# Casting loads for V and K, f32 loads for q, and new instruction lists in a chunk-selecting attention kernel with an ELU layer behind it

## The chip, the core and the metric

The kernel runs on one core of a Trainium2 chip. A core has a matrix engine (TensorE, PE in the profile, with its weight loads as PEld), a vector engine (VectorE, DVE), a scalar engine (ScalarE, ACT), a general engine (GpSimd, POOL) and a queue for transfers (SyncE, SP). Each runs its own list of instructions in order and waits on semaphores for the others. Transfers run on 16 DMA engines. SP and ACT issue plain transfers; GpSimd issues the ones that change the type on the way. The metric is device time in microseconds (us), the median of the runs shown.

## The reference

Four batches, eight heads, 768 positions, head width 64. The keys lie in 24 chunks of 32. For each query an upper bound of its score with every chunk is taken from the chunk's minimum and maximum; of the chunks not later than its own it keeps the six with the largest bound. Softmax attention runs over the kept keys that are not later than the query. The result goes through two dense layers with an ELU between them.

```
k_min, k_max = min and max of k over each chunk
ub  = sum_d max(q_d * k_min_d, q_d * k_max_d)          # chunks later than the query's own: -1e9
sel = the 6 chunks with the largest ub
s   = where(key's chunk in sel and key <= query, q.k / 8, -1e9)
x   = softmax(s) @ v                                   # heads side by side: 3072 x 512
out = elu(x @ w_in) @ w_out                            # w_in 512 x 2048, w_out 2048 x 512
```

All inputs and the output are f32 in memory; the matrix work is done in bf16 apart from transposes and bounds.

## The kernel before

**Units.** A unit is 384 query rows. Units 0 and 1 are the two 192-row halves (called p and s) of the first 384 positions of batches 0 and 1; units 2 and 3 are the second 384 positions of batches 0 and 1; units 4 to 7 are the two halves (h 0 and 1) of batches 2 and 3. Heads go in four pairs r, and pairs in two groups G.

**Per unit.** q and k are transposed so that the head width lies on partitions. For batches 0 and 1 TensorE does it (`prep_pair` L423 and L408, `prep` L564) and DVE takes chunk minima and maxima from the transposed keys (L371). For batches 2 and 3 `keys` (L476) casts each 128-row block of k from its f32 landing buffer into a `kt` tile (`kb`), writes the block's chunk marks beside it (`ky`) and has a transposing DMA put it into the score operand `lhs` (`kd`); the minima and maxima come from a second read of k in chunk form (`kc`, L503 to L523). `select` (L600) makes the bounds (L613), finds the sixth largest (L632) and writes a mask row for each query. Scores (L713, L749, L803), exponentials on ACT (L721, L756, L818, L822), a triangular mask on the diagonal blocks (`tri`, L761 and L835, DVE or POOL: a multiplication with a stored triangle), the product with V (L775, L854), the division (L657, L667), and a turn of the result into the first layer's operand `xt` (L690, from unit 4 on a transposing DMA, L678).

**V.** `load_v` (L465) reads a block of V as f32 by SP into a buffer of class `f`, and `v` (L337 on POOL, L324 on ACT, L326 on DVE) casts it into the product's operand `vext`, which holds a whole batch and has two buffers, so batch 2 takes batch 0's.

**The layers.** `mlp` (L865) does for each unit 16 hidden groups `h` (four matmuls of 384 columns, L872), the exponential `e` on ACT (L879), `m` = exp - 1 on POOL or DVE (L881), `g` on DVE (L885, the bf16 tile `gT`), and for each of three row tiles four output groups `o` (four matmuls of 512 columns, L896). The weights are read and cast to bf16 by POOL's transfers (L295 in three pieces, L301 in four).

**The start.** For the p halves q is read and cast by POOL (`wq`, L388) into the first half of an `f` buffer and transposed as bf16 (L408); k is read as f32 by SP and ACT. 22 `fill` matmuls on zeros (L952) stand among the first instructions of TensorE.

**What sets the order.** Nothing is scheduled at run time. `ORDER` is a written list of (engine, operation), and `PLACES` gives each new buffer its slot in its class, with the number of slots in `BUFS`. The framework adds the waits that follow from reads, writes and the reuse of a slot. So each engine runs its part of the list, and what stands behind a waiting instruction waits too.

Of the kernel before, what the change touches and what calls it, by code (L numbers as in the profile page):

```python
# [9 lines left out]
AOT = mybir.AluOpType  # L10
# [29 lines left out]
G0vS0UD00D01PjXA02D09PjYS0sPjZG0wD06Pj-D0iPj+S0uPk0G0aPk1D0oS0rPk2A0TD0jG0kPk3A0tPk4S0XD03G04Pk5  # L40
Pk6Pk7Pk8D05G0bP1mD0lG0cG0WP1hP1nPk9S2dG0eG0pG0VPkaPkbPkcP0KA0OD0PPkdPkeG0nG0gG0fS2fPkfPkgD0qD0m
P18P0RP0IG0dD0SD0MP0BS0zA0JA1cP0+P1iD0CS0xA0FD19P1oP1jS0ZD10D1aD13S2eD0LS2gA1qA1pA15D11GmCP16P1f
P1sS2MA1lGmBD0ND0DD0GS2PS2tP1xA1gD17G0AG08G0yP1wA1kD12P1rP1yS2ND0QP1tA1AGmDP1VA1vA1zD0-P1BP1CP1W
D1DP24P23D25A1uG0YP27P28D26G07D1EG1eP1PP1GD29P1QP1-D1XA2aG0EP1ZD1+D20P1MP1FP1LG2hD1HP2bG1bG2QD1R
P2zD1IA1YP2mD2AP1JD2nP2HP21S2GD1ND1OA1SP1TA2qD2oS2OA1KD22P2uD1UA2cPmYG0HG2sA2ID2BG0hD2pG2CPn4AmZ
Dm-Dm+Pn0An5PmUGn6An1D2vA2JGmEPmQD2wAmVDbqP3jDn7Gn2Dn3A2DS2RAmRGmWPn8A2rG14D3lA1dPmIG2xAn9D3kD3m
GmFA2yPmMD3nPngGnaDmXAmNGmSDnbAmJPnEA2KGmODmTPnsPnAAnhGmGD3oA2FAnFGmKDniPnkD3pGmHDmPA3qA3sPnoDnj
G3rAntP3FDmLAnpGnGPncA3GGnuDnHPnOAnBGnqDnvAndGnCS2kDnrAnlP3+PnwGneA40DnDS2iP3HDnfP36D38A3IP2VD37
P3ZA3tG2LP4jPnIA3-D2XD2WA2ZS4ZPnPA2EG39GnmA2+G2YP4BA3aDnnPnVA4CD41A4kP4DA4EP31P4hP3ePnJA3fD32D33
A4iAnxGnyD4FPnQD34D3gP3uG3JG35DnzG3cG3bPnWA2SD3wS3dA2-D3vD3yD3xA3iS30PnXPnYD3zD2lS2TG2jD3AA3BPnR  # L50
S4-PnKS4YAnSD3ES4XP3LD3CP4MA3hD4lD3DA4NP42DnZP46S4VP3KP43P4GP48A47P4HG2UP4KA49D4IP3QD4JPnLS4WA4L
# [12 lines left out]
DaWD8lD8EGpEDpFAcWGpQDpRDbmG8nG8qA84A8FDd3ApLDpMDpNPpGPpyApjGpkDplAprP8ID8KD8JScSSaBSaCSpbSaHShF
ApHApzA8HAbnG85GpsG8uD8MDptGpIDpJA81AcYGd0GpADpBPqaAqbPpuPpmApnGpoDppDc+ApvGpwDpxAbpD8LPpSApTDpU
PpWPqeApXGqcD8NA86GpYDpZPq2Pp-Pq6PqiPqjPquPqvD8OScZGc-AbjAaIAq3Ap+Aq7DpVGq0Dq1Dq4Dq5DqdA8PP8TP98
PqkGq8Dq9Ad2AqfGqgDqhSboSaJGaKA8UP99A8GA9aD9bP95A96P8VA8WPqwP8XA8YP91A92P93A94P8ZA8-PqxP8+A90D8R
D8SDaVD8QP9iP9mPakP9wD8vGaXA9jA9xSaDPbxP9uAbyDqyPqlA9vAalD97P9dP9cP9qP9sP9zP9kSfpScRGd5ScTSflSd1
ScUDqmA9nA9tP9AA9BGhID9yD9eD9fA9lA9rP9VA9WPqoD9CPaYP9gD9hP9oA9pP9NPbCA9OP9DPamAanP9PP9-P9EP9+A9Q
P9XPqpP9TGaoAa0A9YDb5GbADbDDb4SblSpaSb6D9FD9GDbFDaZPaeP9JP9RPapP9LA9UA9SDa-D9ZPqqPaaPacPaqDa1A9M  # L70
Pa3A9KPa2Dg0Dd6Db7Db8AafAadAarAabPagPaiAajAahPa8Aa9PdnPbsAbtPbHGasPauPatP9HDa4Da5Pa6PqrGfmAbEAbI
A9IAhGAa+Aa7DbaDb9DavDawAfqAqsDbzDbbDbcDbJPaxDayPd8GbdDd9GdcGdbShBSd4DhCSfnDbwDb0DfoSfrPqEAqFGqG
PqIPbeShvAqJDqKAbfAbuPr8Ar9AbgAbhGraAbGDqHDqLSbrSd7SffSqtDrbDfsGbLPrcArdAbiAhOGreDrfPrkArlPqUAqV
AbvPrgPbMDbNGqWDqXDbOArhAhHProAdaGrmDrnDbPGriDrjGg6DbQPr0PqMPqAGbKArpAbBGrqDrrAr1Gr2AqNGqOAdoAqB
PqQAqRGqSAf+DbRDr3DbSDqPPddAdePrwArxPdiAdjPqYAqZGqCDqDDftDqTGbTGryPr4PrsAbVAr5DbWGq-Dq+DfvPrAPbZ
# [926 lines left out]
```

## Time and profile before

| what | value |
|---|---|
| median of 3 runs | 281.37 us (280.41 to 283.12) |
| the profiled execution | 281.2 us, of which the span is 279.5 us |
| TensorE busy | 267.7 us, 96% of the span |
| VectorE, ScalarE busy | 217.2 us, 217.0 us, 78% each |
| GpSimd busy | 128.1 us, 46% |
| bytes moved | 38.07 MB, mean 136 GB/s |
| granted TensorE clock, mean | 0.98 |

The span is the time between the first and the last instruction of the profiled execution; 1.7 us of that execution lie outside it. A busy share is that of the whole span. A wait is put down to the engine and line that ended it. A DMA share above 1 in a stretch means that the 16 engines' packets overlapped each other there.

### The profile page before, as it was taken

What the parts mean: (1) busy time and instruction counts of PE and PEld (TensorE: products, weight loads), DVE (VectorE), ACT (ScalarE), POOL (GpSimd) and SP (SyncE); (2) the same over time, 40 slices, a digit from 0 to 9 for tenths busy, and PEclk for the clock granted to TensorE, in tenths of its full rate; (3) what the DMA queues carried; (4) which work ended last, traced back from release to release, by engine and by line L of the source; (5) the groups of instructions that cost most, each with busy time, mean ns of one, the idle gap of its engine ahead of it and who ended that gap; (6) DMA issues with size and microseconds to landing.
All of it is one profiled execution on the core that took longest, in us unless ns stands there. A gap on an engine that the chain in (4) does not pass through costs nothing.

```text
span 279.5 us, 6962 instructions
## 1 busy us (share of the span) xinstructions
PE 267.7 (96%) x2458; PEld 165.3 (59%) x2458; DVE 217.2 (78%) x655; ACT 217.0 (78%) x491; POOL 128.1 (46%) x256
## 2 busy tenths in 40 slices
PE   7669999999999999999999999999999999999995
PEld 4457555785466855576655555666655556665553
DVE  4957986889978999789998999579797698424931
ACT  2656987889789998999999859886968579982620
POOL 8883954258522665321585736212541346310410
PEclk9876999999999999999999999999999999999999
DMA  9999999999219899965965589317500210033002
GB/s 147 211 195 210 224 197 185 216 237 248 53 59 220 233 236 196 211 150 111 192 169 114 116 218 224 69 41 135 164 4 1 58 39 4 14 126 90 20 11 101
DMA packets 103747, 38.07 MB, mean 136 GB/s; under 512 B 95136, under 2 KB 99488, under 8 KB 103712
## 3 DMA queue, kind: packets, MB, share of 16 engines
q1 hardware_dynamic: 95696, 32.75, 55.4%
q0 software_dynamic: 6832, 4.59, 10.9%
q10 hardware_dynamic: 1184, 0.30, 0.5%
q8 instruction: 19, 0.31, 0.5%
q14 instruction: 16, 0.13, 0.2%
HBM read 30.41 MB, written 6.29 MB: 131 GB/s over the span
## 4 chain that ended last, share of the span: by engine, by line
PE 75%; DVE 8%; ACT 5%; POOL 2%; issue 2%; DMA 1%; DVEq 0%; ACTq 0%; POOLq 0%
PE bank L896 25%; PE bank L872 24%; PE bank L803 10%; PE bank L854 5%; PE bank L613 3%; PE bank L564 2%; DVE gT L885 2%; ACT pt L818 1%; POOL m L881 1%; PE bank L914 1%; PE bank L690 1%; PE bank L423 1%; ACT e L879 1%; PE bank L775 1%; PE bank L749 1%
## 5 line engine op out<-in xcount | busy, mean ns | idle before, releaser
L872 PE MATMUL bank<-xt,w_in_sb 128*128 128x384 bf16 x512 | 90.2, 328 | 0.3 <-DMA xt<-on 0.2
L896 PE MATMUL bank<-w_out_sb,gT 128*128 128x512 bf16 x368 | 89.3, 379 | 0.0
L881 POOL TENSOR_SCALAR m<-e 128x384 f32<-128x384 f32 x100 | 52.0, 529 | 62.0 <-ACT e L879 51.5
L885 DVE SCALAR_TENSOR_TENSOR gT<-bank,m 128x384 bf16<-128x384 f32 x128 | 65.7, 549 | 9.7 <-POOL m L881 8.4
L879 ACT ACTIVATE e<-bank 128x384 f32<-128x384 f32 x128 | 59.1, 493 | 16.0 <-PE bank L872 13.0
L872 PEld LDWEIGHTS <-w_in_sb 128*128 128x128 bf16 x512 | 49.7, 98 | 35.5 <-issue 4.6
L818 ACT ACTIVATE pt<-bank 128x384 bf16<-128x384 f32 (+1 forms) x144 | 67.1, 547 | 3.6 <-PE bank L803 2.5
L896 PEld LDWEIGHTS <-gT 128*128 128x128 bf16 x368 | 34.6, 97 | 36.1 <-issue 2.2
L803 PE MATMUL bank<-rhs,lhs 96*128 96x384 bf16 (+2 forms) x240 | 42.8, 293 | 1.0 <-DVE on L667 0.5
L835 POOL TENSOR_TENSOR pt<-pt,tri 128x256 bf16<-128x256 bf16 (+1 forms) x18 | 16.4, 916 | 38.5 <-ACT pt L822 23.9
L803 PEld LDWEIGHTS <-lhs 96*128 96x128 bf16 x240 | 21.7, 97 | 13.9 <-issue 0.9
L854 PEld LDWEIGHTS <-pt 128*128 128x128 bf16 x576 | 21.0, 97 | 3.6 <-ACT pt L818 0.2
L854 PE MATMUL bank<-vext,pt 128*128 128x65 bf16 x576 | 22.1, 193 | 0.0
L667 DVE TENSOR_TENSOR on<-bank,rcp 128x384 bf16<-128x384 f32 (+1 forms) x37 | 18.7, 510 | 1.3
L326 POOL CAST rhs<-qt 64x384 bf16<-64x384 f32 x24 | 12.8, 539 | 11.8 <-ACT qt L324 10.8
L324 ACT ACTIVATE o<-bank 128x512 f32<-128x512 f32 (+1 forms) x14 | 8.1, 588 | 13.0 <-PE bank L896 10.1
L657 DVE RECIPROCAL rcp<-bank 128x6 f32<-128x6 f32 (+1 forms) x40 | 7.2, 185 | 13.5 <-PE bank L854 9.0
L371 DVE TENSOR_REDUCE kst<-bank 128x12 f32<-128x384 f32 x32 | 16.5, 548 | 1.3 <-ACT kt L324 0.7
L326 DVE COPY o<-bank 128x512 f32<-128x512 f32 (+1 forms) x11 | 7.2, 665 | 12.2 <-PE bank L896 10.0
L835 DVE TENSOR_TENSOR pt<-pt,tri 128x512 bf16<-128x512 bf16 (+1 forms) x30 | 11.2, 390 | 5.4 <-ACT pt L822 3.6
L324 ACT ACTIVATE rhs<-qt 64x384 bf16<-64x384 f32 x28 | 14.2, 518 | 0.5
L822 ACT ACTIVATE pt<-bank 128x512 bf16<-128x512 f32 x24 | 14.0, 604 | 0.7 <-PE bank L803 0.4
(105 smaller groups left out, 340.1 us busy)
## 6 DMA issues: line engine op xcount, KB each, us to landing
f<-in_v_dram SPq DMA_DIRECT2D x22, 256.0 KB, 4.6
out_dram<-o SPq DMA_DIRECT2D x21, 256.0 KB, 3.4
f<-in_q_dram SPq DMA_DIRECT2D x18, 256.0 KB, 4.7
f<-in_k_dram SPq DMA_DIRECT2D x18, 256.0 KB, 4.6
kc<-in_k_dram SPq DMA_DIRECT2D x8, 384.0 KB, 3.9
w_out_sb<-in_moe_w_out_dram POOLq DMA_DIRECT2D x4, 512.0 KB, 9.0
w_in_sb<-in_moe_w_in_dram POOLq DMA_DIRECT2D x2, 512.0 KB, 8.6
w_in_sb<-in_moe_w_in_dram POOLq DMA_DIRECT2D x1, 1024.0 KB, 13.6
```

The source lines that it names most:

```text
L324: nc.scalar.activation(out=dst, in_=src, func=AF.Copy)
L326: eng[e].tensor_copy(out=dst, in_=src)
L667: nc.vector.tensor_tensor(out=ap(on)[:, 0:nt].rearrange("p q h d -> p h q d"), in0=view()[:, :, :, 0:D], in1=ap(rcp)[:, :, 0:nt].to_broadc ...
L803: nc.tensor.matmul(ap(banks[hd])[:, o + pc:o + pc + wd], lhsT=apl(ls, G)[0:96, pr, hd, P * kb:P * (kb + 1)], rhs=ap(rs)[0:96, hd, c0 - HS ...
L818: lambda e, hd=hd, pt=pt, banks=banks, wtot=wtot: nc.scalar.activation(out=ap(pt)[:, hd, PAD:PAD + wtot], in_=ap(banks[hd])[:, 0:wtot], fu ...
L835: eng[e].tensor_tensor(out=view, in0=view, in1=tri[:, 64:64 + P].rearrange("p (a b w) -> p a b w", a=1, b=1) .to_broadcast([P, 2, len(dg), ...
L854: nc.tensor.matmul(view()[:, hd, qi, :], lhsT=ap(pt)[:, hd, P * qi + off:P * qi + off + P], rhs=ap(vx[b])[:, kb, 2 * r + hd, :], start=(kb ...
L872: nc.tensor.matmul(ap(bank)[:, 0:HS], lhsT=w_in_sb[:, kk, P * fc:P * (fc + 1)], rhs=ap(xT[i, kk]), start=(kk == 0), stop=(kk == NKK - 1))
L879: g.op(f"e{i}.{fc}", (ACT,), lambda e, eb=eb, bank=bank: nc.scalar.activation(out=ap(eb), in_=ap(bank)[:, 0:HS], func=AF.Exp), reads=[(ban ...
L881: g.op(f"m{i}.{fc}", (POOL, DVE), lambda e, eb=eb, mb=mb: eng[e].tensor_scalar(out=ap(mb), in0=ap(eb), scalar1=-1.0, scalar2=1.0, op0=AOT. ...
L885: nc.vector.scalar_tensor_tensor(out=ap(gt), in0=ap(bank)[:, 0:HS], scalar=0.0, in1=ap(mb), op0=AOT.max, op1=AOT.min),
L896: nc.tensor.matmul(ap(bank), lhsT=ap(gts[fc])[:, P * tt:P * (tt + 1)], rhs=w_out_sb[:, fc, :], start=(fc == 0), stop=(fc == NFC - 1))
```

## The change

- **V** of all batches: `load_v` no longer reads f32 by SP and casts. GpSimd issues one casting transfer (`wv`) for each of the 26 blocks, straight into `vext`. The 26 f32 loads and the 26 casts are gone. A transfer into a slot of `vext` has to wait until the slot's former batch has been read for the last time.
- **K** of batches 2 and 3: 12 casting transfers (`wk`) into the `kt` tiles take the place of 12 f32 loads and 12 casts `kb`. `ky` and `kd` stay.
- **q** of the p halves: read as f32 by SP, in place of the four casting transfers `wq`; its transposes run in f32 (the path of L423) in place of bf16. Batch 0's are split in two by heads, like its k.
- **The triangular mask** where GpSimd does it in `attend`: one index select for each diagonal block, with zero written below the diagonal, in place of a multiplication with the stored triangle. DVE's stay.
- **Buffers**: `f` 11 to 9 slots, `gT` 17 to 22.
- **The lists** `ORDER` and `PLACES` are new from the first entry to the last, with other choices of engine: `m` 92 on POOL and 36 on DVE (100 and 28 before), `oh` (the 24 one-hot memsets and one clear) on DVE in place of POOL, `qa` 17 on POOL, 9 on DVE, 30 on ACT (24, 4, 28 before), `on` 39 on DVE and 1 on ACT (37 and 3 before), and others by ones and twos. The number of matmuls of the layers, the scores and the products with V is the same, and 22 fills as before. POOL issues 45 transfers (11 before: `wq` 4, weights 7), SP 32 fewer.

```diff
-BUFS = dict(f=11, ..., gT=17, o=3)
+BUFS = dict(f=9, ..., gT=22, o=3)
...
-                    if (n, u) == ("q", 0):
-                        g.op(f"wq{b}{x}", (POOL,), lambda e, buf=buf, x=x: nc.gpsimd.dma_start(
-                            out=short(buf)[0:T96].rearrange("p (h d) -> p h d", d=D),
-                            in_=q[b, :, T96 * x:T96 * (x + 1)].rearrange("h p d -> p h d")),
-                            writes=[(buf, i) for i in range(NG)], dma=True)
-                        continue
...
-        g.op("qT" + tag, (PE,), tr16 if u == 0 else tr(bq, qf),
-             reads=[(f, G) for f in qf] + [(fixed, "idb" if u == 0 else "idf")], writes=[(bq, 0)])
+        g.op("qT" + tag, (PE,), tr(bq, qf), reads=[(f, G) for f in qf] + [(fixed, "idf")],
+             writes=[(bq, 0)])
...
     def load_v(tag, b, kb, p0, p1):
-        vf = Buf("f")
...
-        dma(lambda: (rows(), v[b, :, P * kb + p0:P * kb + p1].rearrange("h p d -> p h d")),
-            [(vf, 0)], [], f"ldv{tag}")
-        vcast(f"v{tag}", lambda: ap(vx[b])[p0:p1, kb, :, 0:D], rows,
-              [(vf, 0)], [(vx[b], (kb, y, r)) for r in range(NPAIR)
...
+        g.op(f"wv{tag}", (POOL,), lambda e: nc.gpsimd.dma_start(
+            out=ap(vx[b])[p0:p1, kb, :, 0:D], in_=v[b, :, P * kb + p0:P * kb + p1].rearrange("h p d -> p h d")),
+            reads=[(fixed, "vo")],
+            writes=[(vx[b], (kb, y, r)) for r in range(NPAIR)
...
-    def keys(b, h, kf):
+    def keys(b, h):
...
-            g.op(f"kb{tag}{x}", (POOL, DVE, ACT), lambda e, kp=kp, x=x: copy(
-                e, ap(kp)[:, :, 0:D], ap(kf[x]).rearrange("p (h d) -> p h d", h=H)),
-                reads=[(kf[x], 0)], writes=[(kp, 0)])
+            t1 = HS * h + P * x
+            g.op(f"wk{tag}{x}", (POOL,), lambda e, kp=kp, t1=t1: nc.gpsimd.dma_start(
+                out=ap(kp)[:, :, 0:D], in_=k[b, :, t1:t1 + P].rearrange("h p d -> p h d")),
+                writes=[(kp, 0)], dma=True)
...
                 def mask(e, pt=pt, dg=dg):
+                    if e == POOL:
+                        for pc in dg:
+                            part = ap(pt)[:, :, PAD + pc:PAD + pc + P]
+                            nc.gpsimd.affine_select(out=part, in_=part, compare_op=AOT.is_ge, fill=0.0, base=0,
+                                                    pattern=[[0, 2], [1, P]], channel_multiplier=-1)
+                        return
```

More of the change, by code (lines that the diff above doesn't have):

```diff
@@ L332, in halves @@
         return ap(bank)[:, 0:HS].rearrange("p (a s) -> p a s", a=2)
-    def vcast(name, dst, src, reads, writes):
-        def emit(e):
-            if e == POOL:
-                nc.gpsimd.tensor_scalar(out=dst(), in0=src(), scalar1=1.0, scalar2=0.0,
-                                        op0=AOT.mult, op1=AOT.add)
-            else:
-                copy(e, dst(), src())
-        g.op(name, (POOL, ACT, DVE), emit, reads=reads, writes=writes)
     def relu(name, dst, src, reads, writes):
@@ L452, in prep_pair @@
             qq[b, G] = (kt, qh)
-            put("qh" + tag, lambda: ap(qh), lambda: turned(bq), (ACT, DVE), [(bq, 0)], [(qh, 0)])
+            put("qh" + tag, lambda: ap(qh), lambda: ap(bq)[:, 0:HS], (ACT, DVE), [(bq, 0)], [(qh, 0)])
         else:
@@ L544, in prep @@
             for n, cls, src in (("k", "f", k), ("q", "f", q)):
-                for x in range(3):
+                for x in range(3 if n == "q" or b < 2 else 0):
                     ff[b, n, x] = buf = Buf(cls)
@@ L551, in prep @@
                         [(buf, 0)], [], f"ld{n}{b}{h}{x}")
-        kf, qf = [[ff[b, n, x] for x in range(3)] for n in "kq"]
+        kf, qf = [[ff[b, n, x] for x in range(3) if (b, n, x) in ff] for n in "kq"]
         if r == 0:
```

173 lines of the change are left out of this document (79 added, 94 removed).

## The prediction

> **What bounds the kernel now.** I read the page's busy times first, then TensorE's own waits before and after 24 us, then the table of stretches.
>
> ```profile
> PE 267.7 (96%) x2458; PEld 165.3 (59%) x2458; DVE 217.2 (78%) x655; ACT 217.0 (78%) x491; POOL 128.1 (46%) x256
> ...
> PE bank L775 <- POOL vext L337: 2.0, 2, 1.3
> PE bank L408 <- DMA f<-in_q_dram: 1.8, 2, 1.0
> ...
> PE bank L749 <- ACT lhs L324: 0.6, 1, 0.6
> PE bank L803 <- DVE on L667: 0.5, 1, 0.5
> PE bank L803 <- ACT rhs L324: 0.5, 1, 0.5
> ```
>
> The first two rows under the busy times are TensorE's largest waits from 4 to 24 us (3.8 us), the last three its largest from 24 us to the end (1.6 us; each has the sum, the count and the longest). So after 24 us TensorE is the bound, its work does not change, and little more than 1.6 us can be won there. What can be won besides lies in the first 24 us. What can be lost is open: any engine or transfer that comes too late stops TensorE.
>
> ```profile
> core 0: us, PE busy (x) PEld busy (x) DVE busy (x) ACT busy (x) POOL busy (x), PEclk, DMA share, GB/s
> ...
> 30.00:40.00 10.00, 10.00 (x72) 6.42 (x71) 9.25 (x33) 9.32 (x20) 8.37 (x17) 1.00 1.26 208
> 40.00:50.00 10.00, 9.38 (x83) 4.75 (x82) 6.73 (x28) 6.39 (x13) 4.81 (x9) 1.00 1.12 191
> ...
> 70.00:80.00 10.00, 10.00 (x66) 4.88 (x52) 9.71 (x42) 7.40 (x17) 3.49 (x7) 1.00 0.15 34
> ```
>
> The last but one figure is the DMA share. From 30 to 50 us it is above 1, from 70 to 80 it is 0.15: the DMA engines are full while the weights come in. So the early part has two bounds, and what TensorE wins there it may have to give to the transfers.
>
> **The start.** The product with V of the first halves (L775) stopped twice for casts on POOL:
>
> ```profile
> 15.98 0.83 POOL L337 TENSOR_SCALAR vext<-f 128x512 bf16<-128x512 f32 x1
> 17.58 0.64 POOL L337 TENSOR_SCALAR vext<-f 128x512 bf16<-128x512 f32 x1
> ...
> 15.16 2.07 ACT L721 ACTIVATE pt<-bank 128x512 bf16<-128x512 f32 x4 [1.27 <-PE bank L713]
> ...
> 16.86 0.71 PE L775 MATMUL bank<-vext,pt 128*128 128x65 bf16 x18 [1.32 <-POOL vext L337]
> 18.27 1.14 PE L775 MATMUL bank<-vext,pt 128*128 128x65 bf16 x30 [0.70 <-POOL vext L337]
> ...
> 23.95 1.50 PE L872 MATMUL bank<-xt,w_in_sb 128*128 128x384 bf16 x4
> ```
>
> Without the casts, batch 1's products wait for its exponentials, which ended at 15.16 + 2.07 = 17.2, 1.0 us before 18.27. Batch 0's products no longer wait till 16.86 (for the cast that ended there, 15.98 + 0.83), so its divisions on DVE are out of the way when batch 1's come. I take both waits, 2.0 us, for the lead with which the first hidden group starts: 23.95 becomes about 22. The bounds are 1.0 (only batch 1's wait was on the path) and 3.8 (q's waits of 1.8 go as well).
>
> q speaks both ways, and the transfers tell how much:
>
> ```profile
> 11.95 0.92 PE L408 MATMUL bank<-ident_b,f 96*128 96x96 bf16 x8 [0.95 <-DMA f<-in_q_dram]
> ...
> DMA  0000003899999999999999999999999999999999
> ...
> q1 hardware_dynamic: 6100, 1.53, 63.8%
> q0 software_dynamic: 3136, 0.39, 49.2%
> ...
> w_out_sb<-in_moe_w_out_dram POOLq DMA_DIRECT2D x1, 512.0 KB, 12.0
> f<-in_q_dram SPq DMA_DIRECT2D x1, 256.0 KB, 15.5
> ...
> q0 software_dynamic: 2112, 2.10, 78.6%
> q1 hardware_dynamic: 4220, 1.17, 45.3%
> ...
> L388 POOL DMA_DIRECT2D f<-in_q_dram x4 | 3.3, 836 | 0.9 <-POOLq L986 0.9
> L301 POOL DMA_DIRECT2D w_out_sb<-in_moe_w_out_dram x4 | 3.2, 791 | 0.0
> ```
>
> The first row is the last transposes of q; the next three are the transfers of 0 to 12.5 us; the next two those issued near 34 us, the last w_out and a q (latency last); the two after them the shares of POOL's queue (q0) and SP's (q1) from 30 to 46 us. From the transfers to 12.5 us a casting packet of 64 elements takes 0.492 x 12.5 x 16 / 3136 = 31 ns of one DMA engine, a plain f32 one 0.638 x 12.5 x 16 / 6100 = 21 ns. The k and q of the p halves are 6144 packets: 6144 x 21 / 16 = 8.1 us from about 1.9 us (the slices show the first packets there), with the landing about 11 us, against 11.95 for the last q before. The V casts (3072 packets, 6.0 us) are issued behind nine setup steps of about half a microsecond (the select row below has 0.52), from about 6 us, and land by about 16, before the exponentials end. But in the new list q's transposes of batch 1 stand before batch 0's scores; if that q is late, so is everything (a rival below). The f32 transposes themselves cost at most 16 x (291 - 223 ns) = 1.1 us and at least nothing, from these rows:
>
> ```profile
> L423 PE MATMUL bank<-ident_f,f 96*128 96x96 f32 x48 | 7.2, 291 | 0.0
> L408 PE MATMUL bank<-ident_b,f 96*128 96x96 bf16 x16 | 1.5, 223 | 1.9 <-DMA f<-in_q_dram 1.8
> ```
>
> I take nothing: TensorE waits in this stretch in any case; if the waits all went, it would be 1.1.
>
> **24 to 55 us: the lead meets the transfers.** Casting all of V up to the s halves adds 6144 x 10 / 16 = 3.8 us of DMA time, plain q takes 3072 x 10 / 16 = 1.9 away: +1.9 us where the share is above 1.1. The second V stands in POOL's queue behind the last w_out. That was issued at 33.87 and landed 12.0 us later, at 45.9. Behind it come batch 0's cast (1024 packets) and batch 1's (1536): 2.0 and 5.0 us of DMA time, and at POOL's queue's 0.786 us in each us 2.5 and 6.3, so 48.4 and 52.2. They are needed here:
>
> ```profile
> 33.87 0.77 POOL L301 DMA_DIRECT2D w_out_sb<-in_moe_w_out_dram x1
> ...
> 50.78 0.35 PE L775 MATMUL bank<-vext,pt 128*128 128x65 bf16 x6
> ...
> 54.49 0.71 PE L775 MATMUL bank<-vext,pt 128*128 128x65 bf16 x18
> ```
>
> Room of 2.3 us each. A lead of 2.0 just fits if the last w_out lands when it did. The first three are issued earlier in the new list, the last later (behind the first mask on POOL), and V's 1.9 us is added to the queue. So I let 1.4 of the 2.0 us through: **-1.4 us**; ends 0 and -2.3.
>
> **After 55 us.** For the removed work I use busy times from the groups:
>
> ```profile
> L835 POOL TENSOR_TENSOR pt<-pt,tri 128x512 bf16<-128x512 bf16 x7 | 8.3, 1193 | 12.4 <-ACT pt L818 11.4 <-PE bank L854 1.0
> L835 POOL TENSOR_TENSOR pt<-pt,tri 128x256 bf16<-128x256 bf16 x11 | 8.1, 739 | 26.1 <-ACT pt L822 23.9 <-PE bank L854 2.2
> L272 POOL TENSOR_SCALAR_AFFINE_SELECT trineg<-trineg 128x384 bf16<-128x384 bf16 x1 | 0.5, 517 | 0.0
> L881 DVE TENSOR_SCALAR m<-e 128x384 f32<-128x384 f32 x28 | 10.4, 378 | 2.1 <-ACT e L879 1.9
> ```
>
> POOL: 34 more issues at 0.8 us are +27 us; 15 casts of about 0.64 (the 17.58 row) go (-10), and eight `m`, seven `qa`, the one-hots and the cheaper masks (28 selects, each below the 0.52 of a wider one, for 20 multiplications at 0.74 and 1.19) take about as much again away. A few us more in sum, on an engine busy 46%. ACT loses 15 casts, at the same 0.64 some 10 us, and takes about half of that back in other copies. DVE loses eight casts (-5) and gains eight `m` (8 x 0.378 = +3) and the one-hots: about even. None of this is on the path, since TensorE's waits there are so short; the cover is TensorE's queued work, and if an engine came to its limit (DVE is at 9.71 of 10 in one stretch above) a late `g` would cost its lateness. I count 0, with -1.6 and, as the same amount the other way, +1.6 as bounds.
>
> The transfers into place have leads of their own. The shortest is that of batch 0's second half: three casts issued behind the last but few `m` of unit 1, and before the first product that needs them TensorE has nine output groups, one hidden group and eleven scores, by these rows 9 x 0.86 + 0.65 + about 2 = 10.4 us:
>
> ```profile
> 83.10 0.65 PE bank L872 x4
> ...
> 86.25 0.86 PE bank L896 x4
> ```
>
> Three casts take an `e` and an `m` (1.1), an issue of 0.8, some 2 us until packets flow (an estimate from the slices above, which show none before 1.9) and 3 x 2.0: 9.9 us, plus the landing's tail of about 1. I count **+0.6 us** (0 to 2). All other V and K casts come with 12 us or more or singly, so they cost nothing; were this cover gone, each would cost up to its 5 to 6 us of latency.
>
> **Sum.** 281.2 - 1.4 + 0.6 = 280.4, rounded 280.4 us as a profiled execution's time, which is 0.2 below the median of the runs; I predict 280.4. The case's own range is 279 to 281.8.
>
> **Rivals.**
> (a) *V of the s halves comes late* (slower). Place: L775 at 50 to 55 us; cause: the last w_out, now issued behind the first mask on POOL (some 36 us), then three casts in the same queue. With the same 12.0 us it lands at 48; if the three casts get only the share of 0.453 that SP's queue had, they need 11 us: 59, against 54.5, 4.5 us late; at 0.786 they are in time. The middle is +2.3, and with the +0.6 it makes 284.1. It decides once the last w_out lands after about 48. For it: DMA shares above 1.1, a latency of 15.5 in the row above. Against: SP has less to carry then, V being gone from it.
> (b) *GpSimd's issues and DVE's copies exclude each other* (slower). A DVE copy that overlapped a w_out issue took twice its mean:
>
> ```profile
> 27.48 0.84 POOL L301 DMA_DIRECT2D w_out_sb<-in_moe_w_out_dram x1
> ...
> 27.73 0.61 DVE L326 COPY kt<-onehot 128x256 bf16<-128x256 bf16 x1
> ...
> L326 DVE COPY kt<-onehot 128x256 bf16<-128x256 bf16 x4 | 1.2, 317 | 0.0
> ```
>
> That is 0.3 us an issue; 34 more issues are 10 us on DVE if each hits one, and half of it where DVE is above 9.2 of 10: 286. Against: the issue rows are narrow (0.79 and 0.84 on the mean), so POOL itself doesn't suffer. [...]
> (c) *Nothing is won at the start, because q is later.* SP issues ten transfers before batch 1's second q, and q's transposes stand ahead of the scores. At 13 us instead of 11 the scores end 2 us later, the lead is gone, and the transposes' 1.1 us count: 282.3.
> (d) *The lead holds and the later waits go too.* -2.0 at the start, -1.6 from L749 and L803 (ACT freed by its casts): 277.6.
>
> **Chances.** Forecast 0.38, (a) 0.22, (b) 0.08, (c) 0.13, (d) 0.19. A measurement of this kernel can tell about 1% (2.8 us) from no change. Faster by over 1% (under 278.6): (d) with its tail, 0.21. Slower by over 1% (over 284.2): (b), half of (a), and a tail of the others, 0.25. Within: 0.54. The range reaches to (d)'s 277.4 and past (a)'s middle, to 285.4, which leaves out (b), (a)'s upper end and (d)'s lower.
>
> **What will show it.** The first L872 at about 22 us instead of 23.95, with no wait of L775 for V; the last q's transposes by about 11.5; the last w_out landing before 47, L775 at 49 to 49.5; a wait of about 0.6 near 70 us for a V cast; DVE copies near POOL's issues at their old means; POOL busy 122 to 135. I am wrong if L775 waits for V after 48 us, if L881 or L885 wait behind a GpSimd transfer for more than a microsecond in sum, or if TensorE has waits over 3 us in all after 60 us.

## The result, and the profile after

The changed kernel takes 282.98 us (median of 20 runs, 281.25 to 286.09), the kernel before 281.38 us (20 runs, 280.40 to 283.12). The ratio is 1.0055, with a 95% interval from 1.0035 to 1.0075: slower by 0.55%, where I had forecast 280.4. The ratios leave out runs more than 1.5% above the fastest of their kernel (one of 20 here, one of 12 with w_in's third piece early, three of 12 in the last experiment, whose other nine have a median of 280.05); medians and ranges are over all runs. The profiled execution took 283.2 us, of which the span is 281.5 us; before it was 281.2 and 279.5.

Line numbers have moved. The bounds are now L580 (L613 before), the hidden groups L845 (L872), the first halves' product with V L742 (L775), the turn into `xt` L657 (L690) and L645 by transfer (L678), the f32 transposes L393 (L423), memsets L246, the subtraction of the bounds' operand `ks` L360 (L374), w_in's loads L290, w_out's L296, the new V loads L436, the new K loads L448, the selects L800.

From the page of the kernel after (busy us, mean ns, and the idle time ahead with what ended it):

```profile
PE 266.5 (95%) x2458; PEld 165.0 (59%) x2458; DVE 215.8 (77%) x675; ACT 211.5 (75%) x480; POOL 135.8 (48%) x247
...
L845 PE MATMUL bank<-xt,w_in_sb 128*128 128x384 bf16 x512 | 90.2, 326 | 2.7 <-DMA xt<-on 2.4
...
L800 POOL TENSOR_SCALAR_AFFINE_SELECT pt<-pt 128x256 bf16<-128x256 bf16 x28 | 11.2, 415 | 33.9 <-ACT pt L785 12.5
L436 POOL DMA_DIRECT2D vext<-in_v_dram x26 | 22.9, 882 | 1.0 <-PE bank L742 1.0
```

TensorE is still busy for 95% of the span, and the hidden groups have a new line of idle time: 2.4 us behind a transfer into `xt`. TensorE's waits, asked for 4 to 24, 24 to 55, 55 to 160 and 160 us to the end, say where (sum, count, longest):

```profile
PE bank L657 <- ACT on L631: 1.0, 1, 1.0
PE bank L657 <- DVE on L634: 0.8, 1, 0.8
...
PE bank L742 <- ACT pt L688: 0.3, 1, 0.3
...
PE bank L580 <- POOL kst L360: 1.7, 1, 1.7
...
PE bank L657 <- DVE on L634: 0.3, 1, 0.3
PE bank L869 <- DVE gT L858: 0.3, 1, 0.3
PE bank L845 <- DVE o L321: 0.2, 1, 0.2
...
PE bank L845 <- DMA xt<-on: 2.4, 2, 2.0
```

The waits for V (2.0 us of L775) and for q's casting loads (1.8 us of L408) are gone, as meant. Three waits are new: 1.8 us for the divisions at the start, 1.7 us for GpSimd at unit 0's bounds, and 2.0 us (of 2.4) for a transposing transfer. To see what each is worth I matched TensorE's instructions of the two traces operation by operation. The lists differ in TensorE's order too (two transposes of q stand behind the first hidden groups in the new one, and two hidden groups ahead of unit 0's bounds), so the end of one operation can compare unequal work. The rows are operations by whose end TensorE has done the same operations in both kernels; the times are their ends in us.

| operation | before | after | difference |
|---|---|---|---|
| hidden group 3 of unit 0 (ahead of unit 0's bounds) | 27.71 | 26.32 | -1.39 |
| hidden group 9 of unit 0 (behind them) | 31.88 | 32.43 | +0.55 |
| hidden group 0 of unit 1 | 67.62 | 67.76 | +0.14 |
| a score of unit 2 | 83.97 | 83.98 | +0.01 |
| hidden group 2 of unit 4 | 166.51 | 166.77 | +0.26 |
| a V product of unit 6 | 215.61 | 215.75 | +0.14 |
| hidden group 6 of unit 6 (its first) | 224.90 | 226.85 | +1.95 |
| last product | 276.03 | 277.98 | +1.95 |

The loss comes in two places. The lead of the start, 1.39 us in these two executions, is lost at unit 0's bounds, and 1.8 us are lost ahead of unit 6's hidden groups, where the kernels had been within 0.3 us of each other from 67 us on at the rows of the table.

**The first place.** GpSimd's own timeline and, below it, the chain of waits from 15 to 35 us (start, us, what), both of the kernel after:

```profile
17.46 0.72 POOL L436 DMA_DIRECT2D vext<-in_v_dram  x1 [0.99 <-PE bank L742]
18.17 0.78 POOL L290 DMA_DIRECT2D w_in_sb<-in_moe_w_in_dram  x1
25.47 0.13 POOL L246 MEMSET vext<- 64x8 bf16 x1 [6.52 <-DMA vext<-in_v_dram]
...
26.68 1.58 POOL L296 DMA_DIRECT2D w_out_sb<-in_moe_w_out_dram  x2
...
30.20 0.21 POOL L360 TENSOR_TENSOR kst<-kst 128x12 f32<-128x12 f32 x1
```

```profile
17.46 7.89 DMA vext<-in_v_dram
...
25.47 0.14 POOL vext L246
...
26.29 0.45 POOL kst L360 x2
...
30.21 0.20 POOL kst L360
```

At 17.46 GpSimd issues the load of rows 64 to 127 of a V block (`wv0s0`). Next but one in its list stands the memset of those rows' column of ones (`vc0`). The two write different columns, but the memset waits for the load to land, and GpSimd stands still for 6.52 us. Behind it stand two subtractions, three w_out loads, copies, a select, and the last operand of unit 0's bounds (`ks0s0`, 30.20), for which TensorE waits 1.7 us. In the kernel before the same V block was read into an `f` buffer, so the memset had no transfer to wait for.

**The second place.** The chain of waits near 221 us, first of the kernel before, then of the kernel after:

```profile
221.92 2.30 DMA xt<-on
224.21 0.04 issue
224.25 4.55 PE bank L872 x27
```

```profile
221.40 4.76 DMA xt<-on
226.16 0.04 issue
226.20 4.55 PE bank L845 x27
```

The last of unit 6's four transposing transfers is issued 0.5 us earlier than before and takes 4.76 us in place of 2.30. GpSimd's timeline says what is new beside it:

```profile
220.14 1.79 POOL L436 DMA_DIRECT2D vext<-in_v_dram  x2
```

Two loads of batch 3's V, which the products read from 242 us on, are issued in the middle of the four. In the kernel before the last load of V had landed at 135.4.

### The profile page after: what moved, and what is told of

Read it like the earlier page. It is cut to its first block, busy times and chain, and to the rows that moved or that the text cites. A ratio compares the mean times of both kernels' runs of the same rounds, so it can differ in the third digit from the quotient of the medians.

```text
span 281.5 us, 6891 instructions
## 1 busy us (share of the span) xinstructions
PE 266.5 (95%) x2458; PEld 165.0 (59%) x2458; DVE 215.8 (77%) x675; ACT 211.5 (75%) x480; POOL 135.8 (48%) x247
## 4 chain that ended last, share of the span: by engine, by line
PE 70%; DVE 11%; DMA 9%; POOL 6%; issue 2%; ACT 1%; POOLq 0%; DVEq 0%; ACTq 0%
PE bank L869 24%; PE bank L845 19%; PE bank L770 10%; PE bank L827 5%; DMA xt<-on 3%; DVE gT L858 3%; DMA vext<-in_v_dram 3%; DMA kc<-in_k_dram 3%; PE bank L531 3%; POOL m L854 2%; PE bank L742 1%; PE bank L393 1%; DVE kst L357 1%; PE bank L580 1%; PE bank L887 1%
## 5 line engine op out<-in xcount | busy, mean ns | idle before, releaser
L845 PE MATMUL bank<-xt,w_in_sb 128*128 128x384 bf16 x512 | 90.2, 326 | 2.7 <-DMA xt<-on 2.4
L854 POOL TENSOR_SCALAR m<-e 128x384 f32<-128x384 f32 x92 | 47.3, 524 | 58.5 <-ACT e L852 43.0
L845 PEld LDWEIGHTS <-w_in_sb 128*128 128x128 bf16 x512 | 49.2, 98 | 37.7 <-issue 6.4
L770 PE MATMUL bank<-rhs,lhs 96*128 96x384 bf16 (+2 forms) x240 | 42.8, 293 | 0.1
L770 PEld LDWEIGHTS <-lhs 96*128 96x128 bf16 x240 | 21.7, 97 | 14.0 <-issue 0.7
L800 POOL TENSOR_SCALAR_AFFINE_SELECT pt<-pt 128x256 bf16<-128x256 bf16 x28 | 11.2, 415 | 33.9 <-ACT pt L785 12.5
L436 POOL DMA_DIRECT2D vext<-in_v_dram x26 | 22.9, 882 | 1.0 <-PE bank L742 1.0
L634 DVE TENSOR_TENSOR on<-bank,rcp 128x384 bf16<-128x384 f32 (+1 forms) x39 | 19.5, 505 | 1.5 <-DVE rcp L624 0.3
L854 DVE TENSOR_SCALAR m<-e 128x384 f32<-128x384 f32 x36 | 15.0, 423 | 3.2 <-ACT e L852 2.7
L321 POOL CAST rhs<-qt 64x384 bf16<-64x384 f32 x17 | 9.3, 550 | 16.3 <-ACT qt L319 15.8
L321 DVE COPY o<-bank 128x512 f32<-128x512 f32 (+1 forms) x13 | 8.6, 669 | 10.2 <-PE bank L869 8.4
L319 ACT ACTIVATE rhs<-qt 64x384 bf16<-64x384 f32 x30 | 15.5, 519 | 0.4
L319 ACT ACTIVATE o<-bank 128x512 f32<-128x512 f32 (+1 forms) x12 | 7.1, 599 | 11.4 <-PE bank L869 8.5
## 6 DMA issues: line engine op xcount, KB each, us to landing
f<-in_q_dram SPq DMA_DIRECT2D x6, 192.0 KB, 11.2
```

The lines of the kernel that those rows point to most:

```text
L319: nc.scalar.activation(out=dst, in_=src, func=AF.Copy)
L436: g.op(f"wv{tag}", (POOL,), lambda e: nc.gpsimd.dma_start(out=ap(vx[b])[p0:p1, kb, :, 0:D], in_=v[b, :, P * kb + p0:P * kb + p1].rearrange ...
L634: nc.vector.tensor_tensor(out=ap(on)[:, 0:nt].rearrange("p q h d -> p h q d"), in0=view()[:, :, :, 0:D], in1=ap(rcp)[:, :, 0:nt].to_broadc ...
L770: nc.tensor.matmul(ap(banks[hd])[:, o + pc:o + pc + wd], lhsT=apl(ls, G)[0:96, pr, hd, P * kb:P * (kb + 1)], rhs=ap(rs)[0:96, hd, c0 - HS ...
L845: nc.tensor.matmul(ap(bank)[:, 0:HS], lhsT=w_in_sb[:, kk, P * fc:P * (fc + 1)], rhs=ap(xT[i, kk]), start=(kk == 0), stop=(kk == NKK - 1))
L854: g.op(f"m{i}.{fc}", (POOL, DVE), lambda e, eb=eb, mb=mb: eng[e].tensor_scalar(out=ap(mb), in0=ap(eb), scalar1=-1.0, scalar2=1.0, op0=AOT. ...
```

## The experiments

My first theory was that these two waits are the whole loss. Times are medians; the ratios are to runs of the kernel before on the same chip, with their 95% intervals. In the diffs the entries of one engine's list are written by name.

### The memset ahead of the load

```diff
 GpSimd:
-  ... ka01p0 wv0s0 w_in2 vc0 kq ks0s1 ks0p0 w_out0 ...
+  ... ka01p0 vc0 wv0s0 w_in2 kq ks0s1 ks0p0 w_out0 ...
```

> The list of the kernel after, with one entry moved: GpSimd's memset of the corner column of batch 0's V (vc0) stands ahead of the casting load of V's rows 64 to 127 of the same block (wv0s0), not behind it. Theory 1 (the loss lies in two waits that DMAs make; the first is this memset, which waits until 25.35 us for the load of its own tile to land, while GpSimd stands still for 6.52 us): the memset runs at about 17.5, the weight loads w_out0 to 2 are issued near 20 and not from 26.68 to 28.64, ks0s0 is done by 26 and not at 30.41, TensorE's wait of 1.7 us at unit 0's bound products (ub00) goes and they end 1.5 to 2 us earlier than in the kernel after; the loss before unit 6 (2.0 us of waiting for a transposing DMA) stays. Time 280.8 to 281.8 where the kernel after has 283.0. Rival (the place of ks0s0 behind three weight loads, three copies and a select is the loss, not the wait): the wait goes but ub00 ends less than 0.7 us earlier, 282.3 to 283. Rival (the earlier weight loads take the DMA engines from unit 1's q and k): ub00 gains, ub10 or unit 1's first work loses as much, 282.5 to 283.5.

Measured: 281.67 us, ratio 1.0027 (1.0004 to 1.0050), against 1.0055 (1.0035 to 1.0075) for the kernel after: some 0.8 us are back, though the intervals overlap. GpSimd's timeline, and TensorE's waits from 24 to 55 us:

```profile
16.31 0.13 POOL L246 MEMSET vext<- 64x8 bf16 x1 [0.81 <-PE bank L742]
...
23.32 0.38 POOL L360 TENSOR_TENSOR kst<-kst 128x12 f32<-128x12 f32 x2 [4.39 <-DVE kst L357]
...
27.38 0.21 POOL L360 TENSOR_TENSOR kst<-kst 128x12 f32<-128x12 f32 x1
```

```profile
PE bank L845 <- DMA w_in_sb<-in_moe_w_in_dram: 1.9, 1, 1.9
```

The wait at the bounds is gone. GpSimd now waits for DVE's reductions until 23.3, so the w_out loads start at 23.65 and not near 20 as I had expected. The bounds end at 28.44, 2.6 us earlier than in the kernel after, of which 0.96 is an earlier start of this execution. But 1.9 us of a new wait follow at once, for the third piece of w_in, which lands at 31.05 here and at 31.53 in the kernel after. Unit 0's last hidden group ends at 36.69, against 37.49: no more is left there than the earlier start.

### The bounds' operand on DVE, the memset where it was

```diff
-  GpSimd: ... tris2 ks0s0 m0.3 ...
+  DVE:    ... kmin0s0 ks0s0 ...
```

> The kernel after with one subtraction moved from GpSimd to DVE: ks0s0, the last input of unit 0's bound products, directly behind the reductions that make it. GpSimd's stop of 6.52 us at the corner memset stays, and so do the late weight loads. Theory 1 in its narrow form (the stop costs only by ks0s0): ks0s0 is done near 25, the next inputs ks0s1 and ks0p0 at 26.74, TensorE's wait at ub00 (28.4 us) goes, 1.5 to 2 us won as by the moved memset: 280.8 to 281.8. In its wide form (the stop also makes the masks' activations m, the lhs copies and the weight loads of unit 0 late): ub00 gains, but a third or more of it is lost again by 52 us, 282 to 282.7.

Measured: 282.2 us, 1.0037 (1.0014 to 1.0060), not to be told from the kernel after. Of TensorE's timeline this row:

```profile
31.52 4.23 PE L845 MATMUL bank<-xt,w_in_sb 128*128 128x384 bf16 x24 [2.49 <-DMA w_in_sb<-in_moe_w_in_dram]
```

The bounds end at 28.28, and unit 0's last hidden group at 37.34, no better than the kernel after (37.49). What was won at the bounds went into the wait for w_in. So GpSimd's stop was not the only thing that held the lead back: w_in was next in line.

### The two loads away from the transposing transfers

```diff
 GpSimd:
-  ... m5.15 tri3001 tri3000 tri3011 qa0311 qa1312 qa1311 wv310 wv311 m6.6 ...
+  ... m5.15 wv310 wv311 tri3001 tri3000 tri3011 qa0311 qa1312 qa1311 m6.6 ...
```

> The list of the kernel after, with two entries moved: the casting loads wv310 and wv311 are issued near 209 us, in a stretch of 3.47 us in which GpSimd is idle, and have landed by 214, before the transposing DMAs of unit 6's xt (216.8 to 221.4 us) are issued; before they were issued at 220.14 and 221.04, between the third and the fourth. Theory 1 (the second wait is the transposing DMAs that run beside these loads: latencies of 5.45 and 4.76 us for the third and the fourth, 3.71 and 2.30 in the kernel before): the fourth takes 2.3 to 3 us, TensorE's 2.0 us of waiting at 223.9 falls below 0.5, and the time falls by 1.5 to 2.3, to 280.7 to 281.5. Rival (the order of the issues on SyncE, or the state of the DMA engines from other transfers, sets these latencies): the fourth stays above 4 us, 282.5 to 283.3. Rival (the wait goes, but DVE or ScalarE is as late for unit 6): latencies fall, the time by under 0.7.

Measured: 280.66 us, 0.9979 (0.9960 to 0.9999): 2.1 us less than the kernel after. The view of tile `xt` from 214 to 228 us has the four transfers' times from issue to landing, in the kernel after and then in this one:

```profile
DMA to landing us min/median/max: 2.3/4.3/5.4
```

```profile
DMA to landing us min/median/max: 2.3/2.8/3.9
```

The last takes 2.33 us, TensorE doesn't wait, and hidden group 1 of unit 6 ends at 228.28 although this execution was 0.3 us behind the kernel after up to 83 us. The rivals (the order of SyncE's issues, another engine as late) fall.

### Both moves

> Both moves of the two kernels before this one at once. Theory 1: the gains add, 3 to 4 us under the kernel after, 279.0 to 280.0, which is 1.4 to 2.4 under the kernel before (281.4). Rival (something else takes over behind the first wait, so that a lead does not live to the end): not below 280.5.

Measured: 279.8 us (279.42 to 279.97), 0.9947 (0.9924 to 0.9969). The gains of the two moves, 0.28% and 0.76% of the time before, add to 1.04%; measured are 1.08%. Put on top of the other move, the memset's gives 0.32%, so both comparisons give it some 0.8 to 0.9 us, each with an interval that reaches down to about nothing. This version is faster than both kernels. TensorE's waits from 24 to 55 us show that the start is still held back, now in other places:

```profile
PE bank L393 <- ACT rhs L319: 1.2, 1, 1.2
PE bank L393 <- DMA f<-in_q_dram: 0.7, 1, 0.7
```

The first is put down to ScalarE; the k of batch 1's second half landed at 38.60, where TensorE's transposes of it began at 38.74, so I take it for that transfer.

### The two loads added to the kernel before

To see the second mechanism alone I added two loads to the kernel before, at the same place in GpSimd's list, once casting and once as f32.

```diff
+    for i in range(2):
+        g.op(f"dm{i}", (POOL,), lambda e, i=i: nc.gpsimd.dma_start(
+            out=store["kt"][i][:, :, 0:D],    # second kernel: halves of store["kc"][0], f32
+            in_=v[3, :, HS + P * i:HS + P * (i + 1)].rearrange("h p d -> p h d")), ...)
 GpSimd:
-  ... qa0311 qa1312 qa1311 m6.6 ...
+  ... qa0311 qa1312 qa1311 dm0 dm1 m6.6 ...
```

> The kernel before with nothing changed but two casting loads added: GpSimd reads two blocks of 128 rows of batch 3's V into buffers of bf16 that nothing uses any more, directly behind the copies qa (near 220.7 and 221.6 us), where the kernel after has its own two; their data is not used. Theory 1 (loads in flight beside them lengthen the transposing DMAs of unit 6): the transposing DMA issued at 221.9, 2.30 us in the kernel before, takes 4 to 5 us, TensorE waits 1.5 to 2.3 us more at 224 us, and the time is 1 to 2 us above the kernel before, 282.1 to 283.1 where that has 281.1. Rival (the transposing DMAs are late in the kernel after for another reason): 2.3 to 3 us, time within 0.5 of the kernel before.

> The same with the two loads not casting: the same rows as f32, 256 KB each, by GpSimd at the same place into an f32 buffer that nothing uses any more. If any transfer lengthens the transposing DMAs by its share of the engines: 4 to 5 us for the last of unit 6 as with casts, 282.1 to 283.1. If it is the casting that does it (packets of 31 ns on average in the kernel after's software queue against 21 ns in the hardware queue): under 3.5 us, and under 0.8 us more than the kernel before.

Measured: 285.0 us, 1.0138 (1.0107 to 1.0169) with casts, 284.8 us, 1.0120 (1.0088 to 1.0152) with f32 loads. With casts, the chain of waits near 221 us and TensorE's waits from 210 us on:

```profile
222.01 4.22 DMA xt<-on
```

```profile
PE bank L872 <- DMA xt<-on: 1.4, 1, 1.4
```

The same with f32 loads:

```profile
223.01 4.83 DMA xt<-on
```

```profile
PE bank L872 <- DMA xt<-on: 2.0, 1, 2.0
```

The same transfer took 2.30 us without the loads, and TensorE waited 0.2. So loads in flight beside it do this, though GpSimd issues them and SyncE the transfer, and casting is not needed for it. (The 31 and 21 ns of the second expectation are those of the first 12.5 us of the kernel before; in the kernel after its page gives 38.5 ns a packet for the software queue and 30.2 for the hardware queue.) By the matched operations 1.23 and 1.75 us are lost at this place. Both kernels lost more than I expected: in both profiled executions (283.3 and 284.8 us) 1.0 us goes near 96 us, over 120 us ahead of the added loads, where DVE waits for the chunk form of k, and in the second 0.85 us in the first 50. Why is open, and so is why the median of the first (285.0, of four runs) lies 1.7 us above its profiled execution. What these two kernels show is the place and its wait, not the whole of their time.

### w_in's third piece early

```diff
 GpSimd (with both moves):
-  ... w_in0 ks1p1 ka01p0 vc0 wv0s0 w_in2 kq ...
+  ... w_in0 w_in2 ks1p1 ka01p0 vc0 wv0s0 kq ...
```

> The kernel with both moves (279.8 us) with one entry more moved: the third piece of w_in is issued by GpSimd directly behind the first two, near 14 us, and not behind batch 0's V cast at 18.2. In the kernels with the memset moved and with ks0s0 on DVE, ub00 ended 1.6 to 1.8 us earlier than in the kernel after when their earlier starts are taken off, and TensorE then waited 2.06 and 2.65 us for this piece, which landed at 31.05 and 31.48. Theory A (in the first 45 us the DMA engines are the bound, their row shows 9 in all of its first seven slices, so a lead that the start wins is held back by whichever transfer lands next): w_in2 lands earlier by 1 to 3 us, but the loads of batch 1's k and q, or the V casts, land as much later, and the time stays within 0.7 us of 279.8. Rival B (only the place of this piece holds the lead back): ub00 to unit 0's last h run without a wait of 0.5 us, and 278.0 to 279.0.

Measured: 279.57 us, 0.9949 (0.9926 to 0.9973), not to be told from both moves alone. Its timeline of TensorE:

```profile
22.70 2.22 PE L845 MATMUL bank<-xt,w_in_sb 128*128 128x384 bf16 x12
24.76 0.25 PE L393 MATMUL bank<-ident_f,f 96*128 96x96 f32 x1
26.30 0.80 PE L393 MATMUL bank<-ident_f,f 96*128 96x96 f32 x7 [1.29 <-DMA f<-in_q_dram]
```

The wait for w_in is gone; in its place TensorE waits for q of batch 0's second half, which landed at 26.25 where it landed at 24.04 in the kernel after. That is as theory A has it: with the DMA engines full (a share of 1.12 to 1.22 in each stretch of 2 us from 16 to 28), what was moved ahead made the next one late.

### Half of w_in left out

```diff
-            out=w_in_sb[:, :, P * c0:P * c1],   in_=wi[:, :, P * c0:P * c1]
+            out=w_in_sb[:, 0:2, P * c0:P * c1], in_=wi[:, 0:2, P * c0:P * c1]
...
-                lhsT=w_in_sb[:, kk, P * fc:P * (fc + 1)]
+                lhsT=w_in_sb[:, kk % 2, P * fc:P * (fc + 1)]
```

> The kernel with both moves and w_in's third piece early (279.6 us, TensorE waits 1.46 us at 24.76 for q of batch 0's second half, which lands at 26.25 after 14.85 us), with half of w_in's DMA work taken away: only the first two of w_in's four row blocks are loaded, 1 MB less to read and write, and the other two are not computed with; the products of unit h use the first two twice, so that TensorE's work keeps its length. Theory A (the DMA engines bound the first 45 us, so what the start won in the changed kernels is held back there): the wait at 24.76 goes, q lands before 21, w_in's last piece before 27, unit 0's last h ends 1.5 to 2.5 us earlier (36.7 there), and the time is 277.2 to 278.4. Rival (the lead is held back by DVE, ScalarE or the order of the list, which this leaves alone): unit 0's last h within 0.7 us of before, 278.9 to 279.9.

> The same half load in the kernel before. There TensorE comes to unit 0's first h at 23.95, about 1.2 us later than in the kernel after, held by the casts of V, and no row shows it waiting for w_in or for a load between 20 and 35 us. Theory A: little to win, 280.4 to 281.4 where the kernel before has 281.2; so the difference between the two kernels with half the load, 2.5 to 3.8 us, shows what the lead of the start is worth where the DMA engines leave it. Rival (the kernel before is as much bound by its DMA in these 45 us): 279 to 280.

Measured: 279.2 us, 0.9918 (0.9886 to 0.9950) on the changed kernel, 281.25 us, 0.9993 (0.9972 to 1.0014) on the kernel before. The second is as theory A has it: the kernel before wins nothing. The first is not; its 279.2 and the 0.47 us below lie where the rival had them. q landed at 19.81 and w_in's last piece at 24.38, TensorE waited for no transfer from 24 to 55 us, and yet unit 0's last hidden group ended only 0.47 us earlier (36.26 for 36.73). TensorE's timeline has a part of the reason, in the same twelve matmuls as the first row of the last fence, and the table of stretches (the last three figures are granted clock, DMA share, GB/s) confirms it:

```profile
22.07 3.61 PE L845 MATMUL bank<-xt,w_in_sb 128*128 128x384 bf16 x12
```

```profile
22.00:24.00 2.00, 2.00 (x11) 1.04 (x10) 2.00 (x6) 0.69 (x2) 0.44 (x3) 0.68 1.38 193
24.00:26.00 2.00, 2.00 (x10) 1.24 (x9) 1.13 (x3) 1.16 (x3) 2.00 (x4) 0.50 1.30 227
26.00:28.00 2.00, 2.00 (x16) 1.42 (x16) 1.77 (x5) 1.84 (x5) 1.45 (x4) 0.96 1.24 182
```

The granted clock was down: 2 x (0.32 + 0.50 + 0.04) = 1.7 us lost, as much as 3.4 us at half. So in this execution the clock took what the transfers had left free. Of the kernel's six runs, the four with a mean granted clock of 0.994 (this one among them) took 279.19 to 279.61 us, the two with 1.000 took 277.92 and 279.02. How much of the lead could live without both stays open, and so does the rival; with all runs, the two kernels with half the load are 2.0 us apart, where theory A had 2.5 to 3.8.

### Masks by multiplication again

```diff
-                    if e == POOL:
+                    if False:
```

This is the kernel with both moves, with the product on GpSimd too.

> The kernel with both moves, and GpSimd makes its triangle masks again by a product with the table, as the kernel before: 23 products at about 0.67 us for one block and 1.16 for two, for 28 selects at 0.41. GpSimd's busy time rises by some 7 us of 278. Theory (GpSimd has slack wherever it masks, no wait for it of note in the kernel after beyond 30 us): 279.5 to 280.3. Rival (the selects are worth time): above 280.5.

Measured: 280.24 us, 0.9963 (0.9943 to 0.9983), against 0.9947 (0.9924 to 0.9969) with selects, not told apart. From the page:

```profile
PE 264.4 (95%) x2458; PEld 162.9 (58%) x2458; DVE 217.2 (78%) x675; ACT 211.7 (76%) x480; POOL 143.1 (51%) x237
...
L808 POOL TENSOR_TENSOR pt<-pt,tri 128x512 bf16<-128x512 bf16 (+1 forms) x18 | 17.4, 966 | 29.0 <-ACT pt L785 11.3
```

GpSimd works 17.4 us on masks in place of 11.2, and it costs no time that the runs can tell.

### A third place

```diff
 GpSimd (both moves, w_in2 early):
-  ... tri2020 tri2030 wk311 qa1212 qa0211 qa1211 m4.7 wv211 ...
+  ... tri2020 tri2030 qa1212 qa0211 qa1211 m4.7 wk311 wv211 ...
```

> The kernel with both moves and w_in's third piece early, with one casting load more taken out of a stretch of transposing DMAs: wk311 (K of batch 3), which GpSimd issues at 154.58 between the first two and the last two transposing DMAs of unit 4 (latency of the third 4.83 us, 4.05 in the kernel before), goes behind the next m, near 162. Theory: the third takes near 4.1, TensorE comes to unit 4's first h without a wait (0.5 to 1.27 us in four of the kernels so far, under 0.4 in this one): 0 to 0.6 us less, 279.0 to 279.6. Rival (kd311 and the q loads behind it on SyncE now come late for unit 6): above 280.

Measured: 280.68 us (278.75 to 284.68), 0.9957 (0.9924 to 0.9989), not told apart from the 0.9949 without the move. The third transfer fell to 2.34 us, further than I had expected, and TensorE doesn't wait there. But in this execution it lost 0.4 us a little later to GpSimd's copy of the mask rows (`PE bank L770 <- POOL rhs L321`). The time lies where the rival had it, but TensorE shows no wait for `kd311` or a load of q behind it. A gain of this move isn't shown.

## Why the prediction was wrong

**The start: the waits went, the lead was mis-sized.** The product with V waits no longer for a cast, as I said. But "I take both waits, 2.0 us" was wrong: the first hidden group started at 22.79, 1.16 us earlier, near the lower bound of 1.0, and two transposes of q that stood ahead of it now stand behind it. The step that failed is that batch 0's divisions would be "out of the way": one of them ran on ScalarE at 21.24 to 22.17, behind copies of keys, though its products had ended at 17.15. TensorE waits 1.0 us for it, and 0.8 for one of batch 1's, which stands behind a reduction on DVE (the two rows of L657 above). q was not late: its last transfer landed at 11.53 ("about 11"), and TensorE waits for none. The last two transposes of q ended at 12.57 and 14.51, not by 11.5, the second of them because it stands behind batch 0's scores in the list. So what rival (c) has as its cause did not come. And I did not read the clock in the rows that I had. These are of the kernel before, then of the kernel after:

```profile
20.00:22.00 2.00, 2.00 (x16) 1.99 (x17) 1.50 (x5) 1.08 (x5) 0.87 (x4) 0.50 1.22 196
22.00:24.00 2.00, 2.00 (x18) 1.95 (x17) 1.52 (x6) 2.00 (x8) 0.78 (x2) 0.50 1.18 209
24.00:26.00 2.00, 2.00 (x8) 0.93 (x7) 0.82 (x4) 0.79 (x2) 0.51 (x2) 0.51 1.11 217
```

```profile
20.00:22.00 2.00, 0.40 (x4) 0.11 (x2) 1.27 (x5) 1.66 (x6) 0.00 (x0) 1.00 1.21 193
```

The kernel before runs this stretch at half speed with TensorE always busy; the kernel after has the full clock and stands idle. A lead read from waits alone leaves that out. The kernel with the two f32 loads added shows how much: up to those loads, past 220 us, its list is that of the kernel before, and in its execution the clock stayed at 1.00 through the start. TensorE waited 1.5 us for V's casts and 2.0 for q there, and still its first hidden group started at 22.90, 0.11 us behind the kernel after, and hidden group 3 ended at 26.17, where the kernel after has 26.32. So the lead of 1.16 to 1.39 us came mostly from the half clock in the one execution of the kernel before that I had read. How much of it the changed loads give at the full clock is open; one execution of each shows next to nothing.

**"So I let 1.4 of the 2.0 us through": wrong, nothing was let through** (+0.14 at 67.62 us, +0.01 at 83.97). That the transfers can take the lead was seen; the lower end of this term, 0, was right. What I did not see was GpSimd's list: a memset into the tile that a load is writing, with 6.52 us of standing still and the bounds' operand behind it. I had followed what waits for V on TensorE, and not what waits for the V load on the engine that issues it. Taking this wait away gave back some 0.8 us of time, hardly clear of noise; taking the next one (w_in) away too gave nothing that could be measured.

**The V loads of the s halves, and rival (a).** The last w_out landed at 47.35 (before 47, I said), the V loads at 50.43 to 53.38, and TensorE's product began at 51.25, not at 49 to 49.5, with no wait for V. Rival (a) did not decide, because TensorE had lost its lead before.

**"I count +0.6 us" near 70 us: wrong.** TensorE's waits from 55 to 90 us show none. The three loads were issued at 72.39 to 74.22 and landed by 78.52; their product came at 82. I had counted 10.9 us from the `e` to the landing; from the first issue to the last landing it took 6.1. The landing's tail of about 1 us in that count was an estimate with no row behind it; here the last packets ended by 77.90, 0.6 us ahead of the last landing.

**"After 55 us ... I count 0": wrong by the main part of the loss, 1.9 us** (from +0.01 at 84 us to +1.95 at the end, 1.8 of it ahead of unit 6's hidden groups). The step is "the transfers into place have leads of their own": I asked of each load whether it comes in time for its own reader, and not what it does to a transfer of another queue that is short and on the path. I also wrote that I would be wrong if TensorE's waits after 60 us came to more than 3 us; they are 0.8 + 2.4 = 3.2.

**Rival (b)** falls by its size. GpSimd's 26 issues of V took 882 ns on the mean, and most of DVE's work beside an issue keeps its length, but not all of it. Here, near 164 us, the first row is GpSimd's, the others are DVE's:

```profile
163.86 1.79 POOL L436 DMA_DIRECT2D vext<-in_v_dram  x2
```

```profile
163.91 0.36 DVE L854 TENSOR_SCALAR m<-e 128x384 f32<-128x384 f32 x1
...
165.10 1.01 DVE L858 SCALAR_TENSOR_TENSOR gT<-bank,m 128x384 bf16<-128x384 f32 x2
166.09 0.64 DVE L854 TENSOR_SCALAR m<-e 128x384 f32<-128x384 f32 x1
```

The first `m` takes 0.36 us beside an issue, as with GpSimd idle (0.35), and the two `g` 0.51 each (0.549 on the mean before); the second `m`, beside a copy of GpSimd's and the issue at 166.47, takes 0.64. Beside an issue alone one at 175.53 takes 0.56 and a `qr` at 134.60 0.58 in place of 0.25. DVE's `m` rose from 0.378 to 0.423 us on the mean. Over the some 150 rows of DVE that overlap an issue, the excess over their length alone is 1 to 2 us, where (b) had 10, and TensorE's waits for DVE after 60 us come to 0.8. That the two engines exclude each other is not shown: a few rows of DVE are stretched, and GpSimd's own issues stay at 1.02 us or less.

**The rest.** GpSimd is busy 135.8 us, just above the 122 to 135. The time, 282.98, is inside the wide range (277.4 to 285.4; (d), from which its lower end is taken, adds up to 277.6) and above the forecast's own 279 to 281.8. It went the other way: slower, where I had forecast faster. The 280.4 that I forecast is near what the kernel with both moves takes (279.8), but that does not bear the forecast out: its profiled execution ends hidden group 0 of unit 1 at 67.65, level with the kernel before (67.62), and wins its 1.35 us after that, where I counted 0. What wins them is open.

## What to carry to other kernels

When a load is made to write its final tile, look for every small write into the same tile on every engine, and above all on the engine that issues the load, and put them ahead of it: here one memset made GpSimd stand still for 6.52 us. When loads are moved to another queue, look at which short transfers with a reader close behind run beside them, and put the loads into a stretch that has none: here one went from 2.30 us to 4.22 to 4.83 beside two loads. A wait taken away at a stage where the transfers are full can come back as a wait for the next transfer in line, as 1.7 us at unit 0's bounds came back as 1.9 us for w_in's third piece, at DMA shares of 1.1 to 1.5 from 20 to 32 us; so price it from what lands next.

## What the runs showed that I had not expected

- The last transposing transfer of unit 6 takes 2.3 us without GpSimd's loads and 4.2 to 4.8 us beside two loads of 128 rows, whether these cast or not; TensorE's wait for it goes from 0.2 to 1.4 and 2.0 us. Others of these transfers took up to 5.2 us in the kernel before already.
- A memset waits for a transfer into other columns of the same rows (6.52 us), here by the waits that the framework adds.
- The granted clock falls to 0.5 in some executions between 10 and 28 us, in pieces of the same length: 1.7 us are lost at 22 to 28 us in the kernels with the loads apart, with half of w_in, and with the third move, 3.4 us of half clock each; in the profiled executions of the kernel after and with both moves it stays at 1.00 there. In the kernel before two such pieces follow each other from 19 to 26 us, with 3.4 us lost. With half of w_in, TensorE is busy 2.05 of the 4 us ahead of the piece, from 18 to 22 us, and its longest idle time there is 1.02. From run to run of one and the same kernel the clock differs: its mean over the nine runs with both moves goes from 0.985 to 1.000. What decides it was not tested.
- With both waits gone the nine runs lie close together, 279.42 to 279.97 us, against 281.25 to 286.09 in the kernel after; with w_in's third piece early as well they spread again (278.08 to 285.08), so the waits are not shown to be the reason.
